# A token-major W1 product with shifted stationaries, its result transposed by DMA, and a W2 of seven lapped halves

## The chip, the cores and the metric

The kernel runs on one core of a Trainium2 chip. The metric is the device time of one execution in microseconds, taken as the median of several runs.

## What is computed

Two branches read the same normalised input, and their sum is added to the input. Sizes: S = 2048 tokens, D = 448, 16 heads of 28, F = 1792, all in bfloat16.

```python
def reference(A_x, A_wqkv, A_w_phi, A_wo, B_x, B_w1, B_w2, B_w3, B_w4):
    x = A_x
    xn = _layernorm(x)
    return x + _A_ref(xn, A_wqkv, A_w_phi, A_wo) + _B_ref(xn, B_w1, B_w2, B_w3, B_w4)

def _B_ref(x, w1, w2, w3, w4):
    h = _gelu(_layernorm(x) @ w1)
    c = D // 4
    # four groups of c channels, shifted by +1, -1, +2, -2 tokens (zeros move in)
    g0 = pad(h[:, :, 0*c:1*c], token +1); g1 = pad(h[:, :, 1*c:2*c], token -1)
    g2 = pad(h[:, :, 2*c:3*c], token +2); g3 = pad(h[:, :, 3*c:], token -2)
    hs = concatenate([g0, g1, g2, g3], axis=-1) @ w2
    x1 = x + hs
    return x1 + _gelu(_layernorm(x1) @ w3) @ w4
```

`_A_ref` is linear attention: q, k and v from `xn @ wqkv`, feature maps of q and k by softmaxes of `+p` and `-p` (p = q or k times `w_phi`), `kv` summed over all tokens, then numerator over denominator for each token, times `wo`.

## The kernel before

The tokens lie in 16 tiles of 128. `xn` holds the normalised input token-major, `xnT` channel-major: 448 channels as four chunks of 128 partitions of which two pairs overlap by 64 rows ("lapped"). A product over 448 channels is then seven halves of 64 rows. `lap_pair` makes two products at once: one works in rows 0 to 63 of TensorE while the other works in rows 64 to 127, and in its second part the two swap their row groups.

All work goes through a `Recorder`. The order in which operations are recorded is the order on each engine; it finds out which earlier operation each one needs and puts the waits in. It goes by the bytes of a buffer, so two views of one region are told apart only by where they lie. A DMA counts as a reader of its source until it has landed. A matmul that writes a PSUM bank which the other row group has just written waits for that write. The DMA queue of SP (`R.dma`, `R.dma_t` without an engine) takes its instructions in order and waits at each for what it needs.

The stages, in the order in which TensorE has them:

- **First stage**, a list by hand (`play([(xn_T, 0, 0), ...])`): transposes of xn by TensorE for tiles 0 to 11 (`xn_T`), by DMA for tiles 12 to 15 (`xn_Td`); v for the first twelve tiles (`V`); the product with w1 (`W`); the folding of `w_phi` into the weights of q and k (`FO`), which reads the transposed weights `wT`.
- **W1 before** (`w1_pair`, `w1_out`): w1's columns are stationary, 112 at a time, and 512 tokens of `xnT` move. The result is channel-major, 112 channels by 512 tokens, and gelu writes it into `hT`. There are eight pairs of 14 matmuls.
- **Eight passes** (`for ps in range(8)`): each has a k product of two tiles (banks 2 and 3), a q product of two chunks (banks 0 and 1), and at the side a W2 product or a late v product (banks 4 and 5). ScalarE takes exponentials of k (`k_exp`, two for a pass) and of q (`q_exp`, two for a pass, one for each sign). `q_exp` writes into `eq_lo` in passes 0 to 3 and into `eq_hi` after that. From pass 3 on `kv_tile` sums kv.
- **W2 before** (`w2_pair`): stationary is `hT` with the shift in its token index, in four groups of 64 and 48 rows, 16 matmuls for a pair of tiles. `w2_out` adds the result to `xn`.
- **Last stage**, a second list: w3 with gelu, kv's division (`num_tile`), w4 and wo, and the stores.

SP's queue before: loads of x and wv, eight DMA transposes of the weights of q and k into `wT`, four of xn (`xn_Td`), then `load_rest` (w2, w3, wo, w4), later the transposes of `g_tok` and `o_tok` and the stores. A pair's two parts and the exponential of q are these lines:

```python
def q_exp(i, b, s):
    g, c = divmod(i, 4)
    e = (eq_lo if g < 2 else eq_hi)[:, c:c + 2, s, 512 * (g % 2):512 * (g % 2) + 512]
    R.act(e, two(2 * b), ACT.Exp, scale=1.0 - 2.0 * s)
```

Of the kernel before, what the change touches and what calls it, by code (L numbers as in the profile page):

```python
# [5 lines left out]
ACT = mybir.ActivationFunctionType  # L6
# [217 lines left out]
def bass_parallel_sum__linear_kernel_hedgehog__mixer_s_mlp__prompt_kernel(  # L224
    nc, A_x, A_wqkv, A_w_phi, A_wo, B_x, B_w1, B_w2, B_w3, B_w4, out,
):
    _, S, D = A_x.shape
# [3 lines left out]
    NT, NG, KC, NC, NM, FC, HP = 16, 4, 4, 4, 4, 14, 32  # L231
    CR = 112
    SHIFTS = [1, -1, 2, -2]
    HW = S + 16
    x2d, out2d = A_x[0], out[0]

    es = ExitStack()
    with es:
        R = Recorder(nc, es)
        total = [0]  # L240

        def region(name, nbytes):
            nbytes = -(-nbytes // 64) * 64
            total[0] += nbytes
            h = es.enter_context(nc.sbuf_tensor(name, [128, nbytes // 2], BF16))
            R.track(h, nbytes)
            return h

        def view(h, cols, dt=BF16, at=0):
            a = h[:, at // 2:at // 2 + cols * DTB[dt] // 2]  # L250
            return a if dt == BF16 else a.bitcast(dt)

        def new(name, cols, dt=BF16):
            return view(region(name, cols * DTB[dt]), cols, dt)

        pairs = []
        for b in range(4):
            t = es.enter_context(nc.psum_tensor("bank%d%d" % (2 * b, 2 * b + 1), [128, 1024], F32))
            R.track(t, 4096, psum=True)
            pairs.append(t)  # L260
        banks = [pairs[b // 2][:, 512 * (b % 2):512 * (b % 2) + 512] for b in range(8)]
# [1 line left out]

        xtok = new("xtok", NT * D).rearrange("p (t d) -> p t d", t=NT)
        xn = new("xn", NT * 512).rearrange("p (t d) -> p t d", t=NT)
        xnT_r = region("xnT", KC * S * 2)
        xnT = view(xnT_r, KC * S).rearrange("p (c s) -> p c s", c=KC)
        hT_r = region("hT", NM * HW * 2)
        hT = view(hT_r, NM * HW).rearrange("p (m s) -> p m s", m=NM)
        phik_r = region("phik", NT * 1024 * 2)  # L270
        phik = view(phik_r, NT * 1024).rearrange("p (t g e) -> p t g e", t=NT, e=HP)
        vaug_r = region("vaug", NT * 512 * 2)
        vaug = view(vaug_r, NT * 512).rearrange("p (t c) -> p t c", t=NT)
        gT = new("gT", 2 * KC * 512).rearrange("p (b c s) -> p b c s", b=2, c=KC)
        eq_lo = new("eq_lo", NC * 2 * 1024).rearrange("p (c s f) -> p c s f", c=NC, s=2)
        hi_r = region("hi", NC * 2 * 1024 * 2)
        eq_hi = view(hi_r, NC * 2 * 1024).rearrange("p (c s f) -> p c s f", c=NC, s=2)
        wT = view(hi_r, 2 * NC * 512).rearrange("p (t c d) -> p t c d", t=2, c=NC)
# [2 lines left out]
        wpk = new("wpk", KC * D).rearrange("p (c d) -> p c d", c=KC)  # L281
        w1_r = region("w1", KC * D * 2)
        w1 = view(w1_r, KC * D).rearrange("p (c d) -> p c d", c=KC)
        w2 = new("w2", NM * D).rearrange("p (m d) -> p m d", m=NM)
        wo = new("wo", KC * D).rearrange("p (c d) -> p c d", c=KC)
        w3 = new("w3", KC * F).rearrange("p (c f) -> p c f", c=KC)
        w4 = new("w4", FC * D).rearrange("p (c d) -> p c d", c=FC)
# [52 lines left out]
        dve, pool = "DVE", "POOL"  # L340
# [9 lines left out]
        def load_lap(dst, src, engs=("SP", "SP")):  # L350
            for h in range(2):
                R.dma(dst[:, 2 * h:2 * h + 2, :], src[192 * h:192 * h + 256, :].rearrange("(c p) d -> p c d", p=128), engs[h])
# [15 lines left out]
        load_wT(0)  # L368

        def load_rest():  # L370
            R.dma(w2[0:CR, :, :], B_w2.rearrange("(m p) d -> p m d", p=CR))
            load_lap(w3, B_w3)
            load_lap(wo, A_wo)
            R.dma(w4[:, :, :], B_w4.rearrange("(c p) d -> p c d", p=128))
# [10 lines left out]
                                             compare_op=ALU.not_equal, fill=1.0, base=0, channel_multiplier=1),  # L385
             [ident], [ident])
        R.ew(pool, "memset", mhalf[:, :], -0.5)
        R.ew(pool, "memset", hT[:, :, 0:2], 0.0)
        R.ew(pool, "memset", hT[:, :, S + 2:S + 4], 0.0)
        busy = gT[:, 0, 0, 0:256]  # L390
        R.ew(dve, "memset", busy, 1.0)
        R.ew(dve, "memset", vp[:, :, DH + 1:HP], 0.0)
# [14 lines left out]
        def late_3():  # L407
            R.ew(pool, "memset", wpq.rearrange("p c (h e) -> p (c h) e", e=HP)[:, :, DH:HP], 0.0)
            pad = phik.rearrange("p t g e -> p (t g) e")[:, :, DH:HP]
            R.op(pool, lambda e: e.memset(pad, 0.0), [pad], [xn[:, NT - 1, :]])  # L410
            R.ew(pool, "memset", kvq[:, :, :], 0.0)
# [9 lines left out]

        def lap(a):
            return bass.AP(a.tensor, a.offset, [list(a.ap[0]), [192, 2], [1, 256]])

        def halves(a):
            return a.rearrange("p (b e) -> p b e", b=2)
# [21 lines left out]
        def ln1_apply(eng, i):  # L448
            ln_apply(eng, halves(xn[:, i, :]), lap(xtok[:, i, :]), mv, rs, i)
# [38 lines left out]
        def xn_Td(i):  # L488
            R.dma_t(xnT[:, :, 128 * i:128 * i + 128], xn[:, i, :])

        def two(b):
            return pairs[b // 2].rearrange("p (b e) -> p b e", b=2)

        LO, HI = (0, 64), (64, 128)

        def row_pairs(first, second, start=False):
            for s, (p, q) in enumerate(zip(first, second)):
                for out, lhs, rhs in (p, q):
                    R.mm(out, lhs, rhs, start and s == 0, False)

        def lap_pair(outs, lhs, rhs):
            def side(k, rows, kcs):
                return [(outs[k], lhs(k, kc, *rows), rhs(k, kc, *rows)) for kc in kcs]
            return (lambda: row_pairs(side(0, LO, (0, 1, 2, 3)), side(1, HI, (0, 1, 2, 3)), True),
                    lambda: row_pairs(side(1, LO, (0, 1, 3)), side(0, HI, (0, 2, 3))))
# [11 lines left out]
        def v_pair(i, b):  # L517
            return lap_pair([banks[2 * b + k][:, 0:D] for k in range(2)],
                            lambda k, kc, lo, hi: xnT[lo:hi, kc, 128 * (i + k):128 * (i + k) + 128],
                            lambda k, kc, lo, hi: wv[lo:hi, kc, :])  # L520
# [6 lines left out]
            else:  # L527
                R.ew(dve, "tensor_copy", vd, vs)

        def w1_pair(g, m, b):  # L530
            return lap_pair([banks[2 * b + k][0:CR, :] for k in range(2)],
                         lambda k, kc, lo, hi: w1[lo:hi, kc, CR * (m + k):CR * (m + k) + CR],
                         lambda k, kc, lo, hi: xnT[lo:hi, kc, 512 * g:512 * g + 512])

        def w1_out(g, m, b):
            R.act(hT[0:CR, m:m + 2, 2 + 512 * g:2 + 512 * g + 512], two(2 * b)[0:CR, :, :], ACT.Gelu_apprx_tanh)

        def w2_pair(i, b):
            def side(k, lo, hi):
                r = []  # L540
                for m in range(NM):
                    c0 = 2 + 128 * (i + k) - SHIFTS[m]
                    r.append((banks[2 * b + k][:, 0:D], hT[lo:hi, m, c0:c0 + 128], w2[lo:hi, m, :]))
                return r
            return (lambda: row_pairs(side(0, 0, 64), side(1, 64, CR), True),
                    lambda: row_pairs(side(1, 0, 64), side(0, 64, CR)))

        def w2_out(i, b):
            for p0, p1, x0 in ((0, 256, 0), (256, D, 320)):
# [54 lines left out]
        def g_apply(i):  # L604
            ln_apply(pool, halves(g_tok[:, i % 4, :]), lap(xn[:, i, :]), mv2, rs2, i)
# [111 lines left out]
        def play(fs):  # L717
            for f in fs:
                f[0](*f[1:])
# [17 lines left out]
        ln1_stats(15, 1, 0)  # L737
        ln1_apply(dve, 14)
        ln1_apply(dve, 15)
        for i in range(12, NT):  # L740
            xn_Td(i)
        load_rest()
        late_3()

        vps = {i: v_pair(i, b) for i, b in ((0, 2), (2, 3), (4, 3), (6, 2), (8, 2), (10, 3))}
        wps = {(g, m): w1_pair(g, m, b) for g, m, b in ((0, 0, 0), (0, 2, 1), (1, 0, 0), (1, 2, 1), (2, 0, 0),
                                                        (2, 2, 1), (3, 0, 0), (3, 2, 2))}
        fps = {(t, m): fold_pair(t, m, b) for t, m, b in ((1, 0, 2), (1, 2, 3), (0, 0, 1), (0, 2, 3))}

        def V(i, k):  # L750
            return (vps[i][k],)

        def W(g, m, k):
            return (wps[g, m][k],)

        def FO(t, m, k):
            return (fps[t, m][k],)

        spin(19, 256)
        play([(xn_T, 0, 0), (spin, 3, 256), (xn_T, 1, 1), (spin, 4, 256), V(0, 0), (xn_T, 2, 0), V(0, 1), (xn_T, 3, 1),  # L760
              (spin, 2, 256), V(2, 0), (v_out, 0, 2), W(0, 0, 0), (xn_T, 4, 2), V(2, 1), (v_out, 2, 3),
              W(0, 2, 0), (xn_T, 5, 2), W(0, 0, 1), (xn_T, 6, 3), W(0, 2, 1), (xn_T, 7, 2), (w1_out, 0, 0, 0),
              (w1_out, 0, 2, 1), V(4, 0), V(6, 0), V(4, 1), (v_out, 4, 3), V(6, 1), (v_out, 6, 2),
              W(1, 0, 0), (xn_T, 8, 3, 2), W(1, 2, 0), W(1, 0, 1), (xn_T, 10, 3, 2), W(1, 2, 1),
              (w1_out, 1, 0, 0), (w1_out, 1, 2, 1), V(8, 0), V(10, 0), V(8, 1), (v_out, 8, 2), V(10, 1),
              (v_out, 10, 3), W(2, 0, 0), W(2, 2, 0), FO(1, 0, 0), W(2, 0, 1), (w1_out, 2, 0, 0), FO(1, 0, 1),
              FO(1, 2, 0), W(2, 2, 1), (w1_out, 2, 2, 1), FO(1, 2, 1), W(3, 0, 0), FO(0, 0, 0), W(3, 2, 0),
              FO(0, 0, 1), FO(0, 2, 0), W(3, 2, 1), (w1_out, 3, 2, 2), W(3, 0, 1), (w1_out, 3, 0, 0), FO(0, 2, 1)])

        def w2_norm(i):  # L770
            for j in (i, i + 1):
# [6 lines left out]
        side = [("w", 0), ("v", 12), ("w", 2), ("w", 4), ("v", 14), ("w", 6), ("w", 8), ("w", 10)]  # L778
        g_at = {2: (0,), 3: (1,), 4: (2, 3), 6: (4,), 7: (5,)}
        for ps in range(8):  # L780
            k, q = k_pair(2 * ps, 1), q_pair(ps // 2, 2 * (ps % 2), 0)
            kind, i = side[ps]
# [81 lines left out]
        for h in range(2):  # L864
            c = slice(224 * h, 224 * h + 224)
# [32 lines left out]
```

## Time and profile before

| what | value |
|---|---|
| median of 3 runs | 177.84 us (177.82 to 178.65) |
| span of the one profiled execution, first to last instruction | 175.9 us |
| its own time around the span | not recorded; the median is 1.94 us above the span |
| mean granted TensorE clock | 0.999 |
| 512-column matmuls with w1 | 112, 14.8 us busy |
| matmuls with w2 (64 and 48 rows) | 128, 15.0 us busy |
| DMA moved over the span | 14.87 MB, 85 GB/s in the mean |

The profile names a group by engine, operation and tiles (written <- read). PE is TensorE, PEld its weight loads, ACT ScalarE, DVE VectorE, POOL GpSimd, SPq the issuing of DMAs by SP. A timeline's row has its start and length in us from the span's start; rows of one kind are merged, with their count behind the x; in brackets stands how long the engine was idle before, and what ended that. Two things need care: matmuls overlap, so the cost of a group is read from the starts of two groups and not from its length; and a region goes by one name, so a row that names `hi` can be about `wT`.

### The profile page before, as it was taken

To read this page: it belongs to the slowest core of one execution; us is meant where nothing else is said; L and a number is where in the kernel's file an instruction comes from. 1 tells how busy PE (TensorE), PEld (TensorE's weight loads), DVE (VectorE), ACT (ScalarE), POOL (GpSimd) and SP (SyncE) were. 2 spreads that over 40 slices of the span, in tenths; PEclk is the share of its full clock that TensorE was granted. 3 is DMA by queue.
4 is the path that set the end of the run, shared out by engine and by line. 5 is a ranking of instruction groups with operands and counts; after the bars stand their busy time and mean duration, and the time that the engine had idled before them with its cause. 6 is when DMAs were issued, how large, how long until landed. Compare 5 with 4: busy or idle time off the path is not lost.

```text
span 175.9 us, 5042 instructions
## 1 busy us (share of the span) xinstructions
PE 170.8 (97%) x2198; PEld 94.7 (54%) x2198; DVE 110.0 (63%) x252; ACT 82.5 (47%) x92; POOL 93.7 (53%) x130
## 2 busy tenths in 40 slices
PE   7899999998999999999999999999999999999993
PEld 4466557744565555665554554554545545545551
DVE  4799906699899697615776981644427415474621
ACT  2368874997779877926324422223214222224000
POOL 3666670016799999860358489460620723523740
PEclk9999999999999999999999999999999999999999
DMA  5994158990001120121011372134611310311331
GB/s 172 330 240 79 35 97 255 390 345 15 0 4 30 34 60 4 30 55 39 4 34 40 79 74 59 48 82 89 93 30 57 82 34 0 86 30 30 86 100 34
DMA packets 32981, 14.87 MB, mean 85 GB/s; under 512 B 24704, under 2 KB 32448, under 8 KB 32960
## 3 DMA queue, kind: packets, MB, share of 16 engines
q1 hardware_dynamic: 30192, 12.64, 29.6%
q10 hardware_dynamic: 2768, 1.92, 3.4%
q8 instruction: 17, 0.28, 0.7%
q14 instruction: 4, 0.03, 0.1%
HBM read 7.08 MB, written 1.84 MB: 51 GB/s over the span
## 4 chain that ended last, share of the span: by engine, by line
PE 91%; DVE 6%; issue 1%; POOL 0%; ACT 0%; DVEq 0%
PE bank L203 90%; DVE vaug L215 1%; DVE st L215 1%; DVE ksum L215 1%; PE bank L207 1%; DVE xn L215 1%; DVE mv L215 0%; ACT xnT L211 0%; POOL rs L215 0%; DVE rks L215 0%; DVEq L176 0%; DVE gT L215 0%; POOL mv L215 0%
## 5 line engine op out<-in xcount | busy, mean ns | idle before, releaser
L211 ACT ACTIVATE phik<-bank 128x1024 bf16<-128x1024 f32 (+1 forms) x44 | 42.3, 984 | 62.4 <-PE bank L203 62.4
L203 PE MATMUL bank<-gT,w 64*128 64x512 bf16 x392 | 50.1, 377 | 0.0
L215 DVE TENSOR_TENSOR vaug<-bank,vaug 128x464 f32<-128x464 f32 (+3 forms) x65 | 32.6, 512 | 23.0 <-PE bank L203 21.4
L203 PE MATMUL bank<-w,phik 64*128 64x448 bf16 (+1 forms) x420 | 45.0, 349 | 0.0
L215 POOL TENSOR_TENSOR xnT<-vaug 128x196 bf16<-128x196 f32 (+1 forms) x32 | 18.1, 585 | 46.8 <-DVE vaug L215 46.8
L203 PEld LDWEIGHTS bank<-w,phik 64*128 64x128 bf16 (+1 forms) x420 | 21.7, 94 | 21.2 <-issue 0.4
L215 POOL TENSOR_TENSOR phik<-phik,rks 128x1792 bf16<-128x1792 bf16 x8 | 25.7, 3212 | 10.8 <-DVE rks L215 10.8
L203 PEld LDWEIGHTS bank<-gT,w 64*128 64x128 bf16 x392 | 18.6, 94 | 17.0 <-ACT hi L211 0.3
L215 POOL TENSOR_TENSOR vaug<-xn,xtok 128x448 f32<-128x448 bf16 x16 | 16.2, 1031 | 0.2 <-DVE vaug L215 0.2
L215 DVE TENSOR_REDUCE ksum<-phik 128x64 f32<-128x1792 bf16 x8 | 16.0, 2006 | 0.0
L203 PE MATMUL bank<-w,hT 64*128 64x448 bf16 (+1 forms) x128 | 15.0, 349 | 0.5 <-DVE vaug L215 0.5
L215 DVE RECIPROCAL vaug<-bank 128x16 f32<-128x16 f32 x16 | 4.1, 257 | 18.0 <-PE bank L203 18.0
L203 PE MATMUL bank<-xnT,wpq 64*128 64x512 bf16 x112 | 14.9, 376 | 0.0
L203 PE MATMUL bank<-xnT,w 64*112 64x512 bf16 x112 | 14.8, 380 | 0.0
L203 PE MATMUL bank<-wpk,xnT 64*128 64x448 bf16 x112 | 13.4, 349 | 0.0
L203 PE MATMUL bank<-wo,xnT 64*128 64x448 bf16 (+1 forms) x106 | 13.4, 349 | 0.0
L215 DVE TENSOR_TENSOR xn<-bank,xn 128x512 bf16<-128x512 f32 (+1 forms) x16 | 9.2, 616 | 6.3 <-PE bank L203 6.3
L203 PE MATMUL bank<-wv,xnT 64*128 64x448 bf16 x112 | 13.0, 350 | 0.1
L215 POOL TENSOR_TENSOR rs<-mv,mhalf 128x1 f32<-128x1 f32 (+2 forms) x18 | 12.2, 679 | 1.5
L215 POOL TENSOR_SCALAR g_tok<-xn,rs 128x512 bf16<-128x512 bf16 x16 | 12.1, 767 | 0.2
L211 ACT ACTIVATE xnT<-bank 128x512 bf16<-128x512 bf16 x12 | 7.0, 603 | 6.3 <-PE bank L207 6.3
L215 DVE BATCH_NORM_STATS2 st<-xtok 128x6 f32<-128x448 bf16 x16 | 9.8, 615 | 0.0
(62 smaller groups left out, 168.0 us busy)
## 6 DMA issues: line engine op xcount, KB each, us to landing
w<-in_B_w_dram SPq DMA_DIRECT2D x2, 896.0 KB, 7.1
out_dram<-vaug SPq DMA_DIRECT2D x15, 112.0 KB, 1.9
w<-in_B_w_dram SPq DMA_DIRECT2D x1, 1568.0 KB, 12.0
xtok<-in_A_x_dram ACTq DMA_DIRECT2D x2, 448.0 KB, 7.3
xtok<-in_A_x_dram SPq DMA_DIRECT2D x2, 224.0 KB, 5.7
w<-in_B_w_dram ACTq DMA_DIRECT2D x2, 224.0 KB, 5.8
wo<-in_A_wo_dram SPq DMA_DIRECT2D x2, 224.0 KB, 8.4
w<-in_B_w_dram SPq DMA_DIRECT2D x1, 392.0 KB, 3.8
```

The lines of the kernel that those rows point to most:

```text
L203: self.op("PE", lambda e: e.matmul(out, lhsT, rhs, start=start, stop=stop, skip_group_check=True), [out], [lhsT, rhs], tile=self._tile(lhsT))
L207: self.op("PE", lambda e: e.transpose(out, in_, ident), [out], [in_, ident], tile=self._tile(in_))
L211: self.op("ACT", lambda e: e.activation(out, in_, func, **kw), [out], [in_] + aps)
L215: self.op(eng, lambda e: getattr(e, name)(out, *args, **kw), [out], aps)
```

## The change

W1's product is turned round. `xnT` becomes the stationary operand, 128 tokens at a time, and 112 columns of w1 move; each of the four channel groups reads `xnT` at its own token shift, for which `xnT` has 16 columns of zeros at both ends. The result is token-major with the shift in it, 56 matmuls for a pair of tiles. Gelu writes it in lapped form into `h_tok`, and a DMA transpose for each tile (`h_T`) makes `hT`, channel-major and lapped. `h_tok` is a view of the region of `eq_lo`. W2 is then an ordinary `lap_pair` of seven halves, 14 matmuls for a pair of tiles, and w2 is loaded in lapped form by two DMAs.

The hand-written list changes with it: the two parts of a W1 pair mostly follow each other, each pair is followed by its gelu and its two transposes (`WO`), and the DMA transposes of xn's tiles 12 to 15 and `load_rest` (`bulk`) come behind the first two of these pairs.

```diff
-    HW = S + 16
+    PAD = 16
+    HW = S + 2 * PAD
...
-        xnT_r = region("xnT", KC * S * 2)
-        xnT = view(xnT_r, KC * S).rearrange("p (c s) -> p c s", c=KC)
-        hT_r = region("hT", NM * HW * 2)
-        hT = view(hT_r, NM * HW).rearrange("p (m s) -> p m s", m=NM)
+        xnT_r = region("xnT", KC * HW * 2)
+        xnT_p = view(xnT_r, KC * HW).rearrange("p (c s) -> p c s", c=KC)
+        xnT = xnT_p[:, :, PAD:PAD + S]
+        hT = new("hT", KC * S).rearrange("p (c s) -> p c s", c=KC)
...
-        eq_lo = new("eq_lo", NC * 2 * 1024).rearrange("p (c s f) -> p c s f", c=NC, s=2)
+        lo_r = region("lo", NC * 2 * 1024 * 2)
+        eq_lo = view(lo_r, NC * 2 * 1024).rearrange("p (c s f) -> p c s f", c=NC, s=2)
+        h_tok = view(lo_r, NT * 512).rearrange("p (t d) -> p t d", t=NT)
...
-            R.dma(w2[0:CR, :, :], B_w2.rearrange("(m p) d -> p m d", p=CR))
+            load_lap(w2, B_w2)
...
-        R.ew(pool, "memset", hT[:, :, 0:2], 0.0)
-        R.ew(pool, "memset", hT[:, :, S + 2:S + 4], 0.0)
+        R.ew(pool, "memset", xnT_p[:, :, 0:PAD], 0.0)
+        R.ew(pool, "memset", xnT_p[:, :, PAD + S:HW], 0.0)
...
-        def w1_pair(g, m, b):
-            return lap_pair([banks[2 * b + k][0:CR, :] for k in range(2)],
-                         lambda k, kc, lo, hi: w1[lo:hi, kc, CR * (m + k):CR * (m + k) + CR],
-                         lambda k, kc, lo, hi: xnT[lo:hi, kc, 512 * g:512 * g + 512])
+        def w1_pair(i, b):
+            def side(k, rows, kcs):
+                r = []
+                for kc in kcs:
+                    for m in range(NM):
+                        c0 = PAD + 128 * (i + k) - SHIFTS[m]
+                        c = slice(CR * m, CR * m + CR)
+                        r.append((banks[2 * b + k][:, c], xnT_p[rows[0]:rows[1], kc, c0:c0 + 128],
+                                  w1[rows[0]:rows[1], kc, c]))
+                return r
+            return (lambda: row_pairs(side(0, LO, (0, 1, 2, 3)), side(1, HI, (0, 1, 2, 3)), True),
+                    lambda: row_pairs(side(1, LO, (0, 1, 3)), side(0, HI, (0, 2, 3))))
+
+        def w1_out(i, b):
+            R.act(h_tok[:, i:i + 2, :].rearrange("p t (h e) -> p t h e", h=2), lap2(two(2 * b)), ACT.Gelu_apprx_tanh)
+
+        def h_T(i):
+            R.dma_t(hT[:, :, 128 * i:128 * i + 128], h_tok[:, i, :])
...
         def w2_pair(i, b):
-            def side(k, lo, hi):
...
+            return lap_pair([banks[2 * b + k][:, 0:D] for k in range(2)],
+                            lambda k, kc, lo, hi: hT[lo:hi, kc, 128 * (i + k):128 * (i + k) + 128],
+                            lambda k, kc, lo, hi: w2[lo:hi, kc, :])
...
-        for i in range(12, NT):
-            xn_Td(i)
-        load_rest()
         late_3()
...
+        def WO(i, b):
+            return (lambda: (w1_out(i, b), h_T(i), h_T(i + 1)),)
+
+        def bulk():
+            for i in range(12, NT):
+                xn_Td(i)
+            load_rest()
...
+              (spin, 2, 256), V(2, 0), (v_out, 0, 2), W(0, 0), (xn_T, 4, 2), V(2, 1), (v_out, 2, 3),
+              W(0, 1), WO(0, 0), W(2, 0), (xn_T, 5, 2), W(2, 1), WO(2, 1), (bulk,), (xn_T, 6, 3), (xn_T, 7, 2),
+              V(4, 0), V(6, 0), V(4, 1), (v_out, 4, 3), V(6, 1), (v_out, 6, 2),
+              W(4, 0), W(4, 1), WO(4, 0), (xn_T, 8, 3, 2), W(6, 0), W(6, 1), WO(6, 1), (xn_T, 10, 3, 2),
+              V(8, 0), V(10, 0), V(8, 1), (v_out, 8, 2), V(10, 1),
+              (v_out, 10, 3), W(8, 0), FO(1, 0, 0), W(8, 1), WO(8, 0), FO(1, 0, 1),
+              FO(1, 2, 0), W(10, 0), W(10, 1), WO(10, 1), FO(1, 2, 1), W(12, 0), FO(0, 0, 0), W(12, 1), WO(12, 0),
+              FO(0, 0, 1), FO(0, 2, 0), W(14, 0), W(14, 1), WO(14, 2), FO(0, 2, 1)])
```

More of the change, by code (lines that the diff above doesn't have):

```diff
@@ L283, in bass_parallel_sum__linear_kernel_hedgehog__mixer_s_mlp__prompt_kernel @@
         w1 = view(w1_r, KC * D).rearrange("p (c d) -> p c d", c=KC)
-        w2 = new("w2", NM * D).rearrange("p (m d) -> p m d", m=NM)
+        w2 = new("w2", KC * D).rearrange("p (c d) -> p c d", c=KC)
         wo = new("wo", KC * D).rearrange("p (c d) -> p c d", c=KC)
@@ L423, in lap, with lap2 @@
             return bass.AP(a.tensor, a.offset, [list(a.ap[0]), [192, 2], [1, 256]])
+        def lap2(a):
+            return bass.AP(a.tensor, a.offset, [list(a.ap[0]), [512, 2], [192, 2], [1, 256]])
         def halves(a):
@@ L528, in v_out @@
                 R.ew(dve, "tensor_copy", vd, vs)
-        def w1_pair(g, m, b):
-            return lap_pair([banks[2 * b + k][0:CR, :] for k in range(2)],
-                         lambda k, kc, lo, hi: w1[lo:hi, kc, CR * (m + k):CR * (m + k) + CR],
-                         lambda k, kc, lo, hi: xnT[lo:hi, kc, 512 * g:512 * g + 512])
-        def w1_out(g, m, b):
-            R.act(hT[0:CR, m:m + 2, 2 + 512 * g:2 + 512 * g + 512], two(2 * b)[0:CR, :, :], ACT.Gelu_apprx_tanh)
-        def w2_pair(i, b):
-            def side(k, lo, hi):
[L540 to L546, printed above, removed]
+        def w1_pair(i, b):
[14 more added lines that the diff above has]
+            R.dma_t(hT[:, :, 128 * i:128 * i + 128], h_tok[:, i, :])
+        def w2_pair(i, b):
+            return lap_pair([banks[2 * b + k][:, 0:D] for k in range(2)],
+                            lambda k, kc, lo, hi: hT[lo:hi, kc, 128 * (i + k):128 * (i + k) + 128],
+                            lambda k, kc, lo, hi: w2[lo:hi, kc, :])
         def w2_out(i, b):
@@ L739, in bass_parallel_sum__linear_kernel_hedgehog__mixer_s_mlp__prompt_kernel @@
         ln1_apply(dve, 15)
-        for i in range(12, NT):
-            xn_Td(i)
-        load_rest()
         late_3()
         vps = {i: v_pair(i, b) for i, b in ((0, 2), (2, 3), (4, 3), (6, 2), (8, 2), (10, 3))}
-        wps = {(g, m): w1_pair(g, m, b) for g, m, b in ((0, 0, 0), (0, 2, 1), (1, 0, 0), (1, 2, 1), (2, 0, 0),
-                                                        (2, 2, 1), (3, 0, 0), (3, 2, 2))}
+        wps = {i: w1_pair(i, b) for i, b in ((0, 0), (2, 1), (4, 0), (6, 1), (8, 0), (10, 1), (12, 0), (14, 2))}
         fps = {(t, m): fold_pair(t, m, b) for t, m, b in ((1, 0, 2), (1, 2, 3), (0, 0, 1), (0, 2, 3))}
@@ L751, in V, with W @@
             return (vps[i][k],)
-        def W(g, m, k):
-            return (wps[g, m][k],)
+        def W(i, k):
+            return (wps[i][k],)
+        def WO(i, b):
[4 more added lines that the diff above has]
+            load_rest()
         def FO(t, m, k):
@@ L760, in bass_parallel_sum__linear_kernel_hedgehog__mixer_s_mlp__prompt_kernel @@
         play([(xn_T, 0, 0), (spin, 3, 256), (xn_T, 1, 1), (spin, 4, 256), V(0, 0), (xn_T, 2, 0), V(0, 1), (xn_T, 3, 1),
[L761 to L768, printed above, removed]
+              (spin, 2, 256), V(2, 0), (v_out, 0, 2), W(0, 0), (xn_T, 4, 2), V(2, 1), (v_out, 2, 3),
[6 more added lines that the diff above has]
+              FO(0, 0, 1), FO(0, 2, 0), W(14, 0), W(14, 1), WO(14, 2), FO(0, 2, 1)])
         def w2_norm(i):
```

## The prediction

> **What bounds the kernel now.** I read the page first, its busy shares and its chain of waits:
>
> ```profile
> span 175.9 us, 5042 instructions
> PE 170.8 (97%) x2198; PEld 94.7 (54%) x2198; DVE 110.0 (63%) x252; ACT 82.5 (47%) x92; POOL 93.7 (53%) x130
> ...
> PE 91%; DVE 6%; issue 1%; POOL 0%; ACT 0%; DVEq 0%
> ```
>
> TensorE is busy for 97% of the span and is 91% of the chain. A microsecond of TensorE work saved or added should therefore arrive at the end, unless TensorE comes to wait. So I read the timeline of TensorE for prices and for the order of the stages:
>
> ```profile
> 1.25 4.07 PE L203 MATMUL bank<-gT 128*128 128x256 bf16 x19 [1.25 <-DVE gT L215]
> ...
> 18.80 1.70 PE L203 MATMUL bank<-xnT,w 64*112 64x512 bf16 x14
> 20.33 0.40 PE L207 MATMUL bank<-ident,xn 64*128 64x64 bf16 x16
> ...
> 42.84 1.03 PE L203 MATMUL bank<-xnT,wpq 64*128 64x512 bf16 x8
> ...
> 50.67 0.63 PE L203 MATMUL bank<-vaug,phik 64*128 64x62 bf16 x32
> 51.12 0.93 PE L203 MATMUL bank<-wv,xnT 64*128 64x448 bf16 x8
> 51.88 0.74 PE L203 MATMUL bank<-wpk,xnT 64*128 64x448 bf16 x6
> ```
>
> Matmuls are pipelined, so the price of a group is the distance from its start to the next start. W1 (64x512 moving) costs 1.53 us for 14, 109 ns each; a 64x448 one 0.76 us for 8, 95 ns; a 64x62 one 0.45 us for 32, 14.1 ns, with a weight load each. The row at 42.84 is the first half of the q product in the third pass; from there TensorE runs to the end without a wait.
>
> Next come the two queues that the change touches, the SP DMA queue and ScalarE's q exponentials:
>
> ```profile
> 6.29 10.96 SPq L218 DMA_TRANSPOSE hi<-in_A_wqkv_dram  x8
> 20.57 5.48 SPq L218 DMA_TRANSPOSE xnT<-xn  x4
> 26.09 1.63 SPq L221 DMA_DIRECT2D w<-in_B_w_dram  x3
> 27.76 0.98 SPq L221 DMA_DIRECT2D wo<-in_A_wo_dram  x2
> 28.79 0.47 SPq L221 DMA_DIRECT2D w<-in_B_w_dram  x1
> ```
>
> ```profile
> 36.03 1.94 ACT L211 ACTIVATE eq_lo<-bank 128x1024 bf16<-128x1024 f32 x2 [0.17 <-PE bank L203]
> 38.21 1.73 ACT L211 ACTIVATE phik<-bank 128x896 bf16<-128x896 f32 x2 [0.24 <-PE bank L203]
> 40.31 1.94 ACT L211 ACTIVATE eq_lo<-bank 128x1024 bf16<-128x1024 f32 x2 [0.38 <-PE bank L203]
> ```
>
> A transpose occupies SP's issue queue for 1.37 us (10.96/8, 5.48/4), a plain load for about 0.54 us (2.70 us for the five from 26.09 to 28.79 start to start). The last bulk load, w4, is issued at 28.79, and the table of DMA issues gives it 12.0 us to landing: 40.8. The first two q exponentials follow their product by 0.1 us or so.
>
> **W1 on TensorE.** 112 matmuls of 512 columns go: 112 x 109 ns = 12.2 us. 448 of 112 columns come. No row has 112 columns; between the 62-column row (14.1 ns) and the 448-column row (95 ns) the line rises 0.21 ns per column, so 112 columns cost 24.6 ns and 448 of them 11.0 us. Bounds by proportion: 10.6 us (112/448 of 95 ns each) and 11.4 us (112/62 of 14.1 ns each). I take 11.0, by the line between the two rows: -1.2 us. The four-fold number of weight loads is paid for in the 62-column row already, which has one load per 14.1 ns.
>
> The Trainium skill speaks against this part: "TensorE: Matmul & The Clock Gate", "Back-to-back issue gap", gives about 81 ns for each matmul of 128 columns in a stream of loads and matmuls, and 131 ns for 512. By that the part would go from 14.7 to 36 us, an estimate of 22 us lost. The row at 50.67 contradicts it for this kernel's alternating 64-row halves, and the sum goes by the row.
>
> **The swap of halves.** The second half of a W1 pair writes the bank that the other row group just wrote, and the Recorder makes TensorE wait for that. Before, other work lay between the halves. Now W(4), W(6), W(10), W(14) have nothing between. A 62-column matmul takes 188 ns from start to end, so a drain is between 0 and 0.19 us: 0.4 us for four, up to 0.8. It lies ahead of the wait below and is covered by it.
>
> **W2.** 16 matmuls per pair become 14: 16 x 95 ns = 1.5 us less. The part after the row at 42.84 is 13 halves, 13 x 0.095 = 1.24 us; the rest lies ahead of the wait below. The lapped load of w2 (2 x 224 KB for 392 KB) adds one issue of 0.54 us and 56 KB.
>
> **Vector, scalar and Pool work.** The eight gelu activations keep 1024 elements (1025 ns) and only write token-major, the two pad memsets move from hT to xnT near the start (105 ns each): nothing. The memsets run before the first xn exists; uncovered they would cost the change in their length, below 0.1 us. Pool's late memsets, which stood behind the bulk in the listing, share no queue with it and stay.
>
> **The sixteen transposes of h.** This is the large term. They go to SP, which takes instructions in order, and they are placed around the bulk: h_T(0..3), then the four xn transposes and now seven loads, then h_T(4..15). From SP's rows:
> - the weight transposes end at 17.25 (6.29 + 10.96). The gelus of W(0) and W(2) should be done by about 16.5 (the first two gelus ended at 17.6 before and come earlier now), so SP isn't kept by them.
> - h_T(0..3): 4 x 1.37, to 22.7. The xn transposes, 20.57 before, are next, to 28.2. The loads follow to 32.0 (7 x 0.54); they start 2.1 us later than before.
> - h_T(4) is issued at 32.0 and h_T(14), the eleventh, at 45.1 to 45.7 (pitch 1.31 to 1.37). Landing takes 2.4 to 2.7 us unhindered (the transposes of gT and of xn), so h_T(14) lands at 47.5 to 48.4 even with an empty DMA queue.
> - In the same queue stand the loads. Before, they landed in order of issue (issue plus median landing: w3 about 34, wo 36, w4 40.8), so I take it that what is issued behind w4 lands behind it: 40.8 + 2.1 + 0.2 (56 KB more at some 331 GB/s) = 43.1. h_T(4) then lands at about 43.6 and h_T(6) at 44.7, taking 0.55 us for each of a backlog (estimate, from about 0.5 to 0.7 us in which the records of one transpose move).
>
> **Who waits.** h_tok lies in the region of eq_lo. The first q exponential of pass 0 overwrites h_tok tiles 0 and 4, the second 2 and 6; those of pass 1 overwrite 8 and 12, then 10 and 14. The Recorder makes each wait for the transposes that read these tiles. Before, pass 0 wrote at 36.03 and pass 1 at 40.31. Now ScalarE stands at the exponential of pass 0 until 44.7, and behind it in its queue are the k exponentials of pass 1 and the q exponentials of pass 1. TensorE can go on only through the k and v products of pass 1, about to 38; its q product needs banks 0 and 1, which that exponential has to empty. It idles about 7 us.
>
> **After the wait.** q_exp(0) ends at 45.8. TensorE then does q, v, q of pass 1: from 38.02 to 40.11 in the timeline, 2.1 us. At what speed? The only stretch after a long idle in this trace is its beginning, the 19 matmuls at 1.25: 4.07 us, 214 ns for 256 columns or 0.84 ns per column. The 64x448 pairs run at 0.42 ns per column (190 ns). The granted clock reads 1.00 in both, so it doesn't show this. Bounds: no loss, or half speed for 4 us. I take half speed, by the nearest row: 4.1 us instead of 2.1, to 49.9. Then q_exp(1), 1.94 us, to 51.9; h_T(12) and h_T(14) have landed by about 49. Meanwhile TensorE does k, w, k of pass 2 (2.0 us), and its q product starts at 51.9.
>
> The Trainium skill has the same beginning as a rule ("TensorE: Matmul & The Clock Gate", "The HAM clock gate"): half clock after an idle window of about 3.4 us, full clock after as long a busy one. It would make the loss about 1.7 us for one such window, an estimate; no run here shows it after an idle in mid-kernel.
>
> **The sum.** The third pass's q product goes from 42.84 to 51.9: +9.1. What was saved before it is lost in the wait. Behind it, -1.24 from W2. The span goes from 175.9 to 183.8. The runs' median is 177.84, 1.94 above the span of the one profiled execution, so 185.7.
>
> Covered by this wait, and worth money only without it: xn's tile 14, which W(12) now needs for its shifts, lands at about 28.2 against 27.2 (1 us), and w2's second half at about 32.6, needed at some 31 (1.5 us).
>
> **The rivals.**
> - Transposes don't stand behind the loads, only SP's issue limits them: q_exp(0) hardly waits (h_T(6) is issued at 34.7 and lands at 37.2), q_exp(1) waits for h_T(14), 47.5 to 48.4, and ends at 48.5 to 49.4. q of pass 2 is then 5.7 to 6.6 late: 182.3 to 183.2, with a cold TensorE up to 2 us more. For it: transposes are small. Against: the loads' order of landing. 0.2.
> - The queue fills up and SP's transposes are held until the loads are through at about 42: h_T(14) is issued at 56 and lands at 58.5, q of pass 2 at 59.5, 193 us. For it: one weight transpose took 1.9 us to issue. Against: seven issues behind a backlog never stalled. 0.05.
> - TensorE keeps its speed, all else as forecast: q_exp(1) is then set by h_T(14) at about 49, ends at 50, 183.8. 0.15.
> - Faster: the reuse of h_tok doesn't bite, because the transposes land before 38 and 40. Then -1.2 -1.5 +0.4 = 175.5, less up to 2.5 us for the late xn tile and w2: 175.5 to 178. It decides only if ten transposes take SP below 0.6 us each (40 less 2.4, less 32.0, over ten) and pass the loads; the rows have nothing below 1.19. 0.1, half of it within the bound of no change.
>
> **How the numbers follow.** The forecast has 0.5. Slower by over 0.5% is it and the first three rivals, 0.9; faster 0.05, same 0.05 (0.5% of the time, 0.9 us, is about what a measurement can tell here). The range goes from 181.1 to 188.3. The low end is the issue-limited case with every transpose at its median issue time of 1.27 us: h_T(14) lands at 46.3, q_exp(1) ends at 47.4, +4.5 -1.24. The high end has a drain of 0.75 us for each (q_exp(0) ends at 46.4, q_exp(1) at 52.4) and TensorE still at half speed for k, w, k of pass 2, 2.0 us more: q at 54.5, +11.7 -1.24.
>
> **What would show it.** In the profile after: SP's transposes of h as four, then twelve behind the loads from about 32; ScalarE's eq_lo rows with a wait on a DMA, of 8 us in pass 0; TensorE idle from 38 to 46; then double time for some 4 us; W1 rows of 64x112 at about 25 ns apart. No such idle, and a q product of pass 2 before 43, would prove it wrong.

## The result, and the profile after

The kernel with the change takes 193.2 us in the median of four runs (191.1 to 196.3), the kernel before 177.9. The ratio is 1.080, with a 95% interval from 1.074 to 1.087. The forecast was slower, at 185.7 us with a range up to 188.3; the measured time is 4.9 us above that range. (Ratios here leave out disturbed runs, so a median over all runs can differ a little from the ratio times 177.9.)

The page of the changed kernel, its span, TensorE's share and the chain that ended last:

```profile
span 191.2 us, 5703 instructions
PE 173.2 (91%) x2518; PEld 94.4 (49%) x2518; DVE 110.5 (58%) x252; ACT 82.7 (43%) x92; POOL 94.0 (49%) x130
PE 78%; DMA 9%; ACT 7%; SPq 2%; DVE 1%; issue 1%; POOL 0%; DVEq 0%; ACTq 0%
```

The span is 15.3 us longer. TensorE went from 97% to 91% of it, and 9% of the chain is now DMA, which was not in the chain before. SP's queue in the timeline:

```profile
18.39 5.20 SPq L218 DMA_TRANSPOSE hT<-lo  x4
23.63 6.04 SPq L218 DMA_TRANSPOSE xnT<-xn  x4
29.72 2.96 SPq L221 DMA_DIRECT2D w<-in_B_w_dram  x4
32.72 1.32 SPq L221 DMA_DIRECT2D wo<-in_A_wo_dram  x2
34.09 0.47 SPq L221 DMA_DIRECT2D w<-in_B_w_dram  x1
34.60 22.16 SPq L218 DMA_TRANSPOSE hT<-lo  x12
```

Up to 34.6 this is the forecast's order, 2.6 us late. Then come twelve transposes in 22.2 us; from the fifth to the fifteenth issue (34.60 to 54.19) it is 19.6 us, where the forecast had 13.1 to 13.7. The first of them alone, in a narrow window of the same timeline, stands for 7.14 us:

```profile
34.60 7.14 SPq L218 DMA_TRANSPOSE hT<-lo  x1
```

ScalarE and TensorE show who waited (rows `lo` are the q exponentials of passes 0 and 1; the bracket gives the idle time before and its end):

```profile
46.06 2.06 ACT L211 ACTIVATE lo<-bank 128x1024 bf16<-128x1024 f32 x2 [3.74 <-DMA hT<-lo]
54.15 1.02 ACT L211 ACTIVATE lo<-bank 128x1024 bf16<-128x1024 f32 x1 [4.40 <-DMA hT<-lo]
56.74 1.02 ACT L211 ACTIVATE lo<-bank 128x1024 bf16<-128x1024 f32 x1 [1.57 <-DMA hT<-lo]
```

```profile
39.25 0.74 PE L203 MATMUL bank<-w,hT 64*128 64x448 bf16 x5 [1.57 <-issue]
...
48.18 1.39 PE L203 MATMUL bank<-xnT,wpq 64*128 64x512 bf16 x8 [3.44 <-ACT lo L211]
49.36 1.33 PE L203 MATMUL bank<-wv,xnT 64*128 64x448 bf16 x6
50.48 1.49 PE L203 MATMUL bank<-xnT,wpq 64*128 64x512 bf16 x6
...
57.82 1.04 PE L203 MATMUL bank<-xnT,wpq 64*128 64x512 bf16 x8 [3.62 <-ACT lo L211]
```

The q product of pass 1 waited for the exponential of pass 0, and that of pass 2 for that of pass 1, each of which waited for transposes. Where TensorE stands against the kernel before, by the starts of four of its groups and the end of the span:

| TensorE's group | before | after | later by | new since the line above |
|---|---|---|---|---|
| k product, pass 0 | 31.41 | 35.95 | 4.5 | first stage |
| q product, pass 1 | 38.02 | 48.18 | 10.2 | 1.8 at the first W2 pair, the first wait |
| q product, pass 2 | 42.84 | 57.82 | 15.0 | half clock, the second wait |
| q product, pass 3 | 47.65 | 64.13 | 16.5 | half clock |
| end of the span | 175.9 | 191.2 | 15.3 | shorter W2, back |

The clock is in the windows (columns: the stretch, its length, busy time and count by engine, granted clock, DMA share, GB/s):

```profile
48.20:51.70 3.50, 3.50 (x20) 1.36 (x22) 0.97 (x1) 1.54 (x2) 0.79 (x1) 0.58 0.43 86
57.80:61.80 4.00, 3.98 (x26) 1.65 (x28) 2.02 (x3) 2.32 (x3) 0.00 (x0) 0.65 0.01 4
```

In the mean of these two stretches, right after the idle ones, the granted clock is 0.58 and 0.65. The trace's own records of the clock are sharper: 0.50 from 48.73 to 52.14 and from 58.97 to 62.38, 3.41 us each, and 1.00 elsewhere from 4.35 to the end of the work. In the first row's stretch q, v and q of pass 1 take 3.6 us (48.18 to 51.76) instead of 2.1.

### The profile page after: what moved, and what is told of

Read it like the earlier page. It is cut to its first block, busy times and chain, and to the rows that moved or that the text cites. A ratio compares the mean times of both kernels' runs of the same rounds, so it can differ in the third digit from the quotient of the medians.

```text
span 191.2 us, 5703 instructions
## 1 busy us (share of the span) xinstructions
PE 173.2 (91%) x2518; PEld 94.4 (49%) x2518; DVE 110.5 (58%) x252; ACT 82.7 (43%) x92; POOL 94.0 (49%) x130
## 3 DMA queue, kind: packets, MB, share of 16 engines
HBM read 7.14 MB, written 1.84 MB: 47 GB/s over the span
## 4 chain that ended last, share of the span: by engine, by line
PE 78%; DMA 9%; ACT 7%; SPq 2%; DVE 1%; issue 1%; POOL 0%; DVEq 0%; ACTq 0%
PE bank L203 77%; DMA hT<-lo 7%; ACT lo L211 4%; SPq L218 2%; ACT xnT L211 2%; DMA xtok<-in_A_x_dram 1%; ACT phik L211 1%; DVE st L215 1%; ACT vaug L211 0%; PE bank L207 0%; DVE xn L215 0%; POOL rs L215 0%; DVE vaug L215 0%; DVE mv L215 0%; DVEq L176 0%
## 5 line engine op out<-in xcount | busy, mean ns | idle before, releaser
L203 PEld LDWEIGHTS bank<-gT,w 64*128 64x128 bf16 x392 | 17.7, 94 | 17.9 <-ACT phik L211 0.4
L211 ACT ACTIVATE lo<-bank 128x1024 bf16<-128x1024 f32 x16 | 16.2, 1023 | 16.8 <-DMA hT<-lo 9.7
L203 PE MATMUL bank<-xnT,wpq 64*128 64x512 bf16 x112 | 16.8, 411 | 7.1 <-ACT lo L211 7.1
L203 PE MATMUL bank<-w,hT 64*128 64x448 bf16 x112 | 14.1, 356 | 1.8 <-issue 1.6
L203 PE MATMUL bank<-w,xnT 64*128 64x112 bf16 x448 | 14.2, 209 | 1.5 <-ACT xnT L211 1.3
L203 PE MATMUL bank<-wv,xnT 64*128 64x448 bf16 x112 | 13.7, 363 | 1.8 <-ACT xnT L211 1.7
L203 PE MATMUL bank<-wpk,xnT 64*128 64x448 bf16 x112 | 14.5, 369 | 0.0
L203 PEld LDWEIGHTS bank<-w,xnT 64*128 64x128 bf16 x448 | 12.3, 94 | 2.9 <-ACT xnT L211 1.4
L203 PEld LDWEIGHTS bank<-xnT,wpq 64*128 64x128 bf16 x112 | 5.8, 100 | 14.2 <-ACT lo L211 7.9
## 6 DMA issues: line engine op xcount, KB each, us to landing
w<-in_B_w_dram SPq DMA_DIRECT2D x1, 1568.0 KB, 11.4
```

The lines of the kernel that those rows point to most:

```text
L203: self.op("PE", lambda e: e.matmul(out, lhsT, rhs, start=start, stop=stop, skip_group_check=True), [out], [lhsT, rhs], tile=self._tile(lhsT))
L211: self.op("ACT", lambda e: e.activation(out, in_, func, **kw), [out], [in_] + aps)
```

## Experiments

**h_tok in idle bytes.** Its tiles 0 to 7 go to gT's region, which they fill (8 KB of each partition, not its first half), 8 to 15 to the unused half of `hi`; the order of all queues stays.

```diff
-        h_tok = view(lo_r, NT * 512).rearrange("p (t d) -> p t d", t=NT)
+        h_toks = [view(gT_r, 8 * 512).rearrange("p (t d) -> p t d", t=8),
+                  view(hi_r, 8 * 512, at=8192).rearrange("p (t d) -> p t d", t=8)]
...
-            R.dma_t(hT[:, :, 128 * i:128 * i + 128], h_tok[:, i, :])
+            R.dma_t(hT[:, :, 128 * i:128 * i + 128], h_toks[i // 8][:, i % 8, :])
```

> h_tok lies in the first half of gT's region (tiles 0 to 7) and in the free upper half of the region hi (tiles 8 to 15), both idle until long after; all else as in the changed kernel, the order of SP's queue too. Theory A (the q exponentials wait for the transposes that read h_tok, because eq_lo reuses its bytes): both waits of ScalarE on a DMA go, TensorE's idle stretches of 3.4 and 3.6 us in passes 1 and 2 go with the half clock behind them, the q product of pass 2 starts at about 49.3 instead of 57.8, and the time is about 183.3 us: 177.9 for the kernel before, 4.6 for the later end of the first stage, 2 for the wait inside the first W2 pair, less 1.2 for the shorter W2. SP is still held for about 7 us at the fifth transpose. Rival B (the reuse is not the cause; TensorE is slowed by the weight loads and by contention with the transposes): 190 us or more.

183.6 us, 1.028 (1.021 to 1.035). No q exponential waits for a DMA any more, and 9.6 us of the loss are gone though SP's transposes still take as long (the four from 34.46 take 11.7 us):

```profile
34.46 11.69 SPq L218 DMA_TRANSPOSE hT<-gT  x4
44.21 1.94 ACT L211 ACTIVATE lo<-bank 128x1024 bf16<-128x1024 f32 x2 [1.62 <-PE bank L203]
48.50 1.94 ACT L211 ACTIVATE lo<-bank 128x1024 bf16<-128x1024 f32 x2 [0.46 <-PE bank L203]
```

Theory A holds; the reuse of the bytes turned a slow queue into a wait. The q product of pass 2 starts at 51.0, not 49.3: there is a gap in the first W2 pair and half clock behind it.

```profile
39.10 0.74 PE L203 MATMUL bank<-w,hT 64*128 64x448 bf16 x5 [1.49 <-issue]
40.00:43.00 3.00, 3.00 (x18) 1.32 (x16) 0.00 (x0) 1.73 (x2) 0.00 (x0) 0.50 1.10 384
```

The half clock doesn't come in every execution: two of the four runs had a mean clock of 1.00 and took 182.6 and 182.7 us, the profiled one had 0.991 and took 184.5.

**The bulk loads last.** w3, wo and w4 are issued behind the last transpose of h; h_tok stays in eq_lo's region.

```diff
         def load_rest():
             load_lap(w2, B_w2)
+
+        def load_late():
             load_lap(w3, B_w3)
...
+        load_late()
+
         def w2_norm(i):
```

> As the changed kernel, h_tok in eq_lo's region, but w3, wo and w4 are issued behind the last transpose of h; only w2's two loads stay where they were. Theory A with the hold of SP as its larger part (a transpose behind the bulk loads isn't issued until they are nearly through): the fifth transpose takes 1.3 us to issue instead of 7.1, h_T(14) lands at about 46.5, about when pass 1 needs it, and the time is 181.5 to 183.5 us, close to that of the kernel with its own source. If the hold has another cause (the transposes' own backlog, or waiting for gelu), SP is still held behind the fourth or fifth transpose and the time stays above 188 us.

186.0 us, 1.035 (1.026 to 1.044, and by this ratio 184.1 us): a clear gain, but above the 181.5 to 183.5 expected. SP's queue, the last exponential of pass 1 and the q product behind it:

```profile
32.52 18.76 SPq L218 DMA_TRANSPOSE hT<-lo  x12
51.27 1.02 ACT L211 ACTIVATE lo<-bank 128x1024 bf16<-128x1024 f32 x1 [1.60 <-DMA hT<-lo]
52.34 1.89 PE L203 MATMUL bank<-xnT,wpq 64*128 64x512 bf16 x8 [3.43 <-ACT lo L211]
```

No transpose is held for 7 us (the first three take 5.7 us together), so the hold came from the bulk loads. But the pitch is 1.56 us (18.76/12), not 1.31, and in the profiled run, the slowest of its four (188.6 us; the others 183.4 to 186.4), the last exponential of pass 1 still waited 1.6 us for its transpose and TensorE 3.4 us for it.

**Both edits.**

> Both edits: h_tok in idle bytes, and w3, wo and w4 behind the last transpose of h. Theory A: nothing waits for the transposes any more, whatever SP does: as the better of the two single edits or up to 1.5 us faster, 181 to 183 us; what is left over the kernel before (about 4 us) is the first stage, where xn's copies queue behind the gelus on ScalarE. If the wait inside the first W2 pair (1.6 us) comes from the bulk loads, it is gone here. Rival B: 188 us or more.

181.4 us, 1.019 (1.014 to 1.024), as expected. Nothing waits for a transpose. The gap in the first W2 pair is absent here, which the expectation had as the sign that it comes from the bulk loads:

```profile
36.99 1.13 PE L203 MATMUL bank<-w,hT 64*128 64x448 bf16 x8 [0.22 <-ACT hi L211]
```

The k product of pass 0 starts at 35.82, 4.4 us late, so what is left over is the first stage:

```profile
15.54 0.42 PE L207 MATMUL bank<-ident,xn 64*128 64x64 bf16 x10 [0.71 <-issue]
16.43 2.82 PE L203 MATMUL bank<-wv,xnT 64*128 64x448 bf16 x28 [0.48 <-ACT xnT L211]
22.48 1.73 PE L203 MATMUL bank<-w,xnT 64*128 64x112 bf16 x53 [1.28 <-ACT xnT L211]
26.31 2.07 PE L203 MATMUL bank<-wv,xnT 64*128 64x448 bf16 x20 [1.11 <-ACT xnT L211]
```

Three waits, 2.9 us together, are for ScalarE's copies of xnT, which now stand behind a gelu in ScalarE's order. The first gap has no releaser at all.

**TensorE kept busy in its idle time.** `fill(n)` is n pairs of 64-row matmuls of 256 columns, on a constant and into two idle banks.

```diff
             for s in range(2):
                 k_exp(2 * ps, 1, s)
+            if ps in (1, 2):
+                fill(30 if ps == 1 else 45)
             q[0]()
```

> The changed kernel with 30 pairs of 64-row matmuls of 256 columns put before the q product of pass 1 and 45 pairs before that of pass 2; they work on a constant into two idle banks and fill most of TensorE's idle time there (about 3.2 and 4.8 us). Theory C (the idle stretches cost a half-rate clock afterwards): the granted clock stays at 1.00 behind them, the second stretch's loss of about 1.7 us goes, the first one's is hidden by the wait for the last transposes: 191.5 us against 193.2. Rival: the half rate is not from idling, and the time stays at 193 us or grows by up to 3 us where the fill outlasts the wait.

193.6 us, 1.084 (1.078 to 1.090): no faster than the change, against the forecast by theory C. In the parts:

```profile
50.40:52.60 2.20, 2.18 (x22) 1.08 (x24) 0.54 (x1) 1.58 (x2) 0.22 (x1) 1.00 0.41 84
60.80:62.80 2.00, 1.97 (x20) 0.99 (x22) 0.32 (x1) 1.59 (x2) 0.00 (x0) 1.00 0.03 8
```

In the profiled run the clock stays at 1.00, and from the q product of pass 2 to that of pass 3 it takes 4.63 us (60.83 to 65.46) instead of 6.31: 1.7 us, as expected. So the half rate comes from idling. The transposes were 3 us later in the profiled run: 1.75 us of it before the fill, when SP's first transpose of h began (20.14 against 18.39), the rest behind it. Whether the fill had a part in that rest isn't settled, and the total is no proof of a gain: of the four runs the two with a mean clock of 1.00 took 192.6 and 194.3 us, and the other two had 0.982 and 0.989 in spite of the fill.

**No transposes of h.** hT is zeros, filled once.

```diff
+            R.ew(pool, "memset", hT[:, :, :], 0.0)
...
-            return (lambda: (w1_out(i, b), h_T(i), h_T(i + 1)),)
+            return (lambda: w1_out(i, b),)
```

> The changed kernel without its sixteen transposes of h: hT is filled with zeros once by Pool in its idle time, so the W2 products multiply zeros; all other work is there. What it shows is the price of the transposes as a whole, on SP, on ScalarE's wait and on the weight loads behind them. Theory A: the price is all but the first stage's lateness; the weight loads start 5 us earlier, W2's wait goes, the q product of pass 2 starts at 47 to 48 and the time is 181 to 182.5 us, as in the kernel with both edits. Rival B (token-major W1 itself is the larger price): 186 us or more.

183.3 us, 1.030 (1.027 to 1.032), 0.8 us above what was expected: the transposes as a whole cost 9.9 of the 15.3 us (193.2 less 183.3). The miss is informative:

```profile
34.44 0.27 PE L203 MATMUL bank<-w,xnT 64*128 64x112 bf16 x4 [0.92 <-issue]
38.63 0.54 PE L203 MATMUL bank<-w,hT 64*128 64x448 bf16 x3 [0.26 <-issue]
40.67 0.74 PE L203 MATMUL bank<-w,hT 64*128 64x448 bf16 x5 [1.50 <-issue]
```

The gap in the first W2 pair is here too, though w2's loads are issued at 28.4 and have 2.9 us to landing. So w2 isn't its cause.

**The bulk loads on ScalarE's queue**, beside the transposes of h on SP's.

```diff
-            load_lap(w3, B_w3)
+            load_lap(w3, B_w3, ("ACT", "ACT"))
...
+              ... W(10, 1), WO(10, 1), (load_act,), FO(1, 2, 1), ...
```

> The changed kernel with w3, wo and w4 issued from ScalarE's queue behind the gelu of W(10), at about 33 us, so that they run on the other DMA queue beside the transposes of h; w2 stays on SP. Two readings of the 7 us for which SP was held at the fifth transpose: if it is the place in the same queue, no transpose of h takes over 2.8 us to issue, h_T(14) lands by 49 and the time is 184 to 188 us (the five issues on ScalarE put off two gelus by up to 2.5 us); if it is that the 16 DMA engines are full, a transpose is held for several us here too and the time is 189 us or more.

190.3 us, 1.067 (1.063 to 1.071), the second reading. One transpose took 3.42 us to issue, and the twelve 22.1 us, as long as behind the loads in one queue:

```profile
34.37 3.42 SPq L218 DMA_TRANSPOSE hT<-lo  x1
```

```profile
32.92 22.12 SPq L218 DMA_TRANSPOSE hT<-lo  x12
```

Another queue brings only 2.9 us: while the loads run, transposes are issued slowly. What inside the DMA hardware holds SP wasn't tried further and stays open. In this run w2's second half did come late, as a wait on a DMA of 2.18 us.

**The first stage in another order**, on top of both edits: the copies of xnT ahead of the gelus, W1 pairs interleaved, and `bulk` behind the first two transposes of h. Of the list these two lines show it; the others are changed in the same way.

```diff
...
-              W(4, 0), W(4, 1), WO(4, 0), (xn_T, 8, 3, 2), W(6, 0), W(6, 1), WO(6, 1), (xn_T, 10, 3, 2),
+              W(4, 0), (xn_T, 10, 2, 2), W(6, 0), W(4, 1), WO(4, 0), W(6, 1), WO(6, 1),
...
```

> The kernel with both edits (h_tok in idle bytes, w3, wo and w4 last), and the first stage's list in another order: xn's transposes and their copies stand ahead of the gelus that they queued behind, two W1 pairs are interleaved so that other work lies between the halves, and xn's tiles 12 to 15 go to SP behind the first two transposes of h. Theory A: TensorE's waits for ScalarE's xnT copies (0.5, 1.3 and 1.1 us) go, the first k product starts at 32.2 to 33 us instead of 35.8, and the time is 177.7 to 178.7 us, level with the kernel before (177.9). Rival: the first stage is bound by ScalarE and by gaps that TensorE has with nothing to wait for, and the time stays at 180 us or more.

179.2 us, 1.0058 (1.0035 to 1.0081): 2.2 us less, but 0.5 above the expected range. Two new waits appeared, 0.54 us for the copy of v and 1.29 us for the normalisation of xn's tile 10, besides gaps of 0.60 and 0.57 us without a releaser.

**A second order.** xn's tiles 8 to 11 are transposed in and behind the W(4) pair.

```diff
-              W(4, 0), (xn_T, 10, 2, 2), W(6, 0), W(4, 1), WO(4, 0), W(6, 1), WO(6, 1),
-              V(8, 0), V(10, 0), V(8, 1), (v_out, 8, 2), V(10, 1),
+              W(4, 0), (xn_T, 8, 3, 2), W(4, 1), (xn_T, 10, 2, 2), WO(4, 0), W(6, 0), V(8, 0), W(6, 1), WO(6, 1),
+              V(10, 0), V(8, 1), (v_out, 8, 2), V(10, 1),
```

> As the reordered kernel, with xn's tiles 8 to 11 transposed inside and behind the W(4) pair instead of ahead of it, where TensorE had waited 0.5 us for the copy of v and 1.3 us for the normalisation, and with v products between the halves of W(6). Theory A: these 1.8 us go, 177.3 to 178.0 us, level with the kernel before or up to 0.3% faster. Rival: the first stage is held by something else by then (ScalarE's copies, or gaps of TensorE with nothing to wait for), and the time stays at 178.7 us or more.

177.9 us against 178.3 for the kernel before beside it, 0.998 (0.996 to 0.9999): level with it (at the interval's best end 0.4% faster, which is no clear gain). From the page and the timeline:

```profile
span 175.7 us, 5704 instructions
PE 168.9 (96%) x2518; PEld 93.5 (53%) x2518; DVE 110.0 (63%) x252; ACT 82.5 (47%) x92; POOL 93.9 (53%) x130
```

```profile
43.99 1.03 PE L203 MATMUL bank<-xnT,wpq 64*128 64x512 bf16 x8
```

The q product of pass 2 is 1.15 us later than before the change (42.84) and the rest 1.35 us shorter (175.7 - 43.99 = 131.7 against 133.1).

**Gaps without a releaser.** The kernel before, with 200 pairs of very short matmuls in its first stage (64 rows, 64 columns, on a constant).

```diff
+              (fill, 200), V(4, 0), V(6, 0), ...
```

> The kernel before, with 200 pairs of 64-row matmuls of 64 columns put behind the first W1 products (on a constant, into banks that are idle then). At 28 ns for a pair they take 5.6 us. Theory D (TensorE uses up its instructions faster than they are fetched when matmuls are this short): inside the burst or right behind it TensorE stands still once or more for 0.3 to 2 us with nothing to wait for, its end some 1.2 to 1.5 us behind the end of a 16 KB transfer on the instruction queue, and the run takes 6 to 9 us more than the kernel before. Rival (the gaps seen after the change belong to it alone): no such gap, 5 to 6 us more.

One run, 188.9 us: 10.6 us over the kernel before, more than the 6 to 9 expected, with this in the timeline:

```profile
16.01 3.12 PE L203 MATMUL bank<-gT 64*128 64x64 bf16 x201 [0.69 <-ACT xnT L211]
21.28 2.04 PE L203 MATMUL bank<-gT 64*128 64x64 bf16 x128 [2.15 <-issue]
25.28 1.22 PE L203 MATMUL bank<-gT 64*128 64x64 bf16 x71 [1.96 <-issue]
```

Between two gaps are exactly 128 matmuls, with their 128 weight loads 256 instructions. The records of the instruction queue have 16 KB transfers that end at 19.8 and 23.9; TensorE goes on 1.5 and 1.4 us after them. In the changed kernel one ends at 37.70 and the gap in the W2 pair at 39.25, 1.55 us later. The place of the gaps says the same. Counting the instructions that the trace has for TensorE, the gaps of the burst come after 705 and 961, those at 15.59 and 39.25 in the changed kernel after 449 and 1473, and those at 34.44 and 40.67 in the kernel without transposes of h after 1217 and 1473: all lie whole multiples of 256 apart. So the gaps are TensorE running out of instructions, and a kernel without the change has them when its matmuls are short enough. The Trainium skill has the block ("Runtime: NRT & Kernel Launch", "Instruction fetch mechanics": refill in 16 KiB blocks of 256 instructions) and calls the cost mostly hidden; here a block of short matmuls costs 4.0 us from start to start (21.28 to 25.28) for 2.0 us of work.

The bulk loads have a part in the gap of the W2 pair. In the changed kernel the 16 KB that end at 37.70 begin 0.9 us after the k product of pass 0; with the bulk loads last they begin 1.3 us before that product, and with both edits 1.5 us before it. The gap is 1.57, 0.47 and 0 us.

## Why the prediction was right and wrong

**Right: the wait and its place.** The q exponentials of passes 0 and 1 wait for the transposes that read h_tok, TensorE behind them, and with idle bytes as the source the wait is gone. The order of SP's queue and the start of its fifth transpose (32.0 forecast, 34.6 measured) were near. So was the landing behind the loads: w4 landed 11.4 us after its issue, at 45.5, and h_T(4) at 46.0, forecast 43.1 and 43.6.

**Wrong: the issue of the transposes behind the loads.** The step that failed is "h_T(14), the eleventh, at 45.1 to 45.7 (pitch 1.31 to 1.37)". It priced the issue by rows whose transposes had no bulk load in flight. Here the first one was held for 7.14 us and the others came at 1.3 to 1.9; h_T(14) was issued at 54.2 and landed at 56.7, 7 to 8 us later than the forecast's 49. So the q product of pass 2 began at 57.8 and not at 51.9, which is 5.9 of the 7.5 us that the forecast was off; the second stretch of half clock, 1.5 us, is nearly all the rest. That hold stood in the text as a rival, at 0.05 and with 193 us. That its time is so close is partly luck: the hold was shorter than it said (h_T(14) at 54.2 and not 56), and the second half clock isn't in it. What stood against it, "seven issues behind a backlog never stalled", was about plain loads, of which the kernel before has six. With the loads last the hold goes; on another queue it stays, spread over several transposes. So it isn't a matter of standing behind them alone.

**Wrong: what the wait covers.** The forecast took the first stage as hidden and counted 1 us for xn's tile 14 and 1.5 for w2. The first stage really ended 4.5 us later, by the copies of xnT queued behind gelus (three waits, 3.0 us) and by instruction fetch (0.55 us at 15.59), neither of which is in the text; what is left is not taken apart. It is also why ScalarE waited 3.7 us in pass 0 and not 8, and TensorE 3.4 and not 7: both came later to a wait that ended at 46.1, forecast 44.7. In the changed kernel the transposes' wait does cover most of that: taking the wait away brought 9.6 of 15.3 us. But for the faster rival ("175.5 to 178") it was decisive: without the wait the kernel is at 183.6, and it takes the loads last and two new orders of the list to reach 177.9.

**Wrong cause, right size by luck: w2.** In the first W2 pair 1.5 us were forecast, for w2's second half landing late, and 1.57 us came. The run without transposes has the gap with w2 long there; it is instruction fetch, put off by the bulk loads.

**Half clock: right in mechanism.** Forecast: half rate for some 4 us after the first idle, from the slow start of the trace. Measured: a clock of 0.50 for 3.41 us each, after both idle stretches, and 1.00 when they were filled. The second one, 1.5 us (the pass to the next q product in the table), isn't in the forecast, which had no second idle stretch; the range's upper end had 2.0 us more of half speed there, as a longer first one. The Trainium skill's rule for it ("TensorE: Matmul & The Clock Gate", "The HAM clock gate", an idle window of about 3.4 us) fits the idle stretches of 3.4 and 3.6 us. It isn't the whole: in the kernel with h_tok in idle bytes a gap of 1.5 us in a thinly used stretch was enough for a clock of 0.50 from 39.86 to 43.27. TensorE was busy for 16% and 34% of the 3.41 us ahead of the two half-clock stretches of the changed kernel, and for 50% ahead of that one. No 3.41 us at full clock that were busy for 55% or more had half clock behind them, nor had one of 45% (35.52 to 38.94, with the loads on ScalarE's queue), so where the line lies isn't settled.

**W1: right on streaming, wrong on the sum.** Forecast 24.6 ns for a matmul of 112 columns; in the changed kernel 55 of them take 1.38 us (12.49 to 13.87), 25.1 ns. With the swap of halves uncovered, 56 take 1.61 us (19.23 to 20.84), the drain being 0.2 us: a pair costs 1.61 where 14 matmuls of 109 ns cost 1.53. For all 448 matmuls with four such drains that is 12.0 us against 12.2, and instruction fetch comes on top. The gain of 1.2 us is not there.

**W2: right.** From the q product of pass 2 to the end the kernel with both edits takes 131.7 us (179.3 - 47.6) instead of 133.1: -1.4, forecast -1.24. In the changed kernel half clock took it back.

## What to carry to other kernels

Before a transfer is given a buffer that is idle "by then", find the engine that next writes those bytes and work out when the last reader's transfer lands in its queue's order; the price of a late one is paid by everything behind that writer. A DMA transpose issued while bulk loads run can cost several times its unhindered issue time (7.1 and 3.4 us here against 1.3), whichever queue the loads are on, so put the loads behind it. Many short matmuls are not priced by their columns alone: they can outrun the fetch of their own instructions, which bulk loads put off further. And what stands behind them on the evacuating engine decides when the next stage can begin.

## What was not expected of the hardware

- A DMA transpose behind 4.3 MB of loads (the seven of the bulk) kept SP for 7.14 us, where the plain loads behind loads took 0.5 to 1.3 us each; beside 3.8 MB on another queue, up to 3.4 us.
- TensorE used up 256 instructions of short matmuls in 2.0 us and then stood 2 us until 1.4 to 1.5 us after the end of the next 16 KB of instructions.
- The clock goes to 0.50 for 3.41 us at a time in mid-kernel, after stretches of the same length in which TensorE was busy for 16 to 50% of the time. In the first microseconds of the span, where 256 columns took 214 ns, twice the usual time, the column reads 1.00, but it can't show the slow start: the trace's records of the clock begin only at 4.35 us in the changed kernel and at 5.01 us in the one before.
